# Two-stage kernel (talking-heads attention, then a squared-ReLU feed-forward): 64-row matmuls in four 64x64 tiles between 64x64 units, and a new order of TensorE's units

## The chip, the cores and the metric

The kernel runs on one core of a Trainium2 chip. The metric is device time in microseconds (us) of one execution, as the median of several runs; lower is better. The profile of one further execution is read beside it. In its rows PE is TensorE's matmuls, PEld its weight loads, DVE is VectorE, ACT ScalarE, POOL GpSimd, and SP the engine that issues part of the transfers. L1230 is line 1230 of the kernel.

## What is computed

```python
def _attn_ref(q, k, v, w_pre, w_post):          # q, k, v: 8 batches, 12 heads, 448 rows, 64 columns
    scores = scale * np.matmul(q, k.transpose(0, 1, 3, 2))
    scores = np.einsum('bhij,hg->bgij', scores, w_pre)
    scores = scores - np.max(scores, axis=-1, keepdims=True)
    attn = np.exp(scores)
    attn = attn / (np.sum(attn, axis=-1, keepdims=True) + 1e-09)
    attn = np.einsum('bhij,hg->bgij', attn, w_post)
    return np.matmul(attn, v)

def _moe_ref(x, w_in, w_out):                   # x: 3584 x 768, w_in: 768 x 2048, w_out: 2048 x 768
    h = np.maximum(x @ w_in, 0.0)
    return h * h @ w_out
```

The output of the attention, heads side by side, is the x of the feed-forward. Scores are mixed over heads before the softmax (w_pre) and after it (w_post).

## The kernel before

The 8 batches are worked through in overlap: while one batch is in attention, an earlier one is in the feed-forward. TensorE's work is cut into 966 units of one or a few dozen matmuls each. They fall into ten streams, each with a fixed order of its own:

- T (stream 0): transposes of q and k, 28 matmuls of 64x64 each. Two evacuations copy the result to `qkt`.
- QK (1): q times k transposed for one pair of heads and a tile of 128 (or, for the last tile of a batch, 64) rows, 448 columns. Two heads lie on the two halves of the 128 rows of the array, since a head has only 64 columns to contract over. `emit_QK`, matmul at L935. Its results are copied to `stage`, and from there SP moves them into the ring `dring`, where the 12 heads of five rows lie side by side.
- pre (2): mixes heads with `wk1`, 4 matmuls of 60 or 64 rows, two chunks at a time. L1004. ACT takes the exponential of the result, with row sums, into `pring` (L1022); DVE takes the reciprocals (L1046); POOL folds them into the weights of the second mix, `wk2s` (L1053).
- post (3): mixes heads after the softmax, 16 matmuls of 60 columns. L1085. Results are copied to `a2t`.
- AV (4): the product with v. One part (`avq`, L1142) uses 64x64 tiles, the rest (L1163) 128x64. Results are copied to `xt`.
- dir (5): batch 0's way to the mixed scores without the ring, full 128x128 matmuls. L883.
- F1 (6, 7): x @ w_in. Batches 0 and 1 use full matmuls (L1209), the later ones pairs of 64 rows (L1230): each unit, called a phase, contracts one half of the rows into one bank and the other half into another, and the second phase swaps them. ReLU and square follow on ACT and DVE (`h1t`, `h2t`).
- F2 (8, 9): h2 @ w_out, in the same paired form (L1351), the last two tiles of the last batch in full matmuls (L1300). The result goes to `osb` and out to memory.

A unit has a form, which the code calls its mode: "full" (128x128), "row" (two tiles of 64x128), "cols" (two of 128x64) or "quad" (four of 64x64). Where the form changes from one unit to the next, the planner adds a fixed time, `MODE_SWITCH`.

The order in which TensorE runs the units is written out by hand as a string, `ORDER`, of one digit per unit: the digit names the stream whose next unit comes. A planner, `_Plan`, lays the program out when the kernel is built: `run` takes units from the string, and at the same time chooses the order on all other engines by estimated costs and priorities, which engine (ACT or DVE) does each evacuation, and which of the eight banks of PSUM each group of results gets. `next_unit` gives the earliest start of the next unit, `_commit_pe` places it. So a new string also gives new queues on ACT, DVE, POOL and SP. Loads of q and k for a batch are released by certain pre units of the batch before; `load_v` and the moves into the ring are released in the same way.

The planner also counts TensorE's instructions and lets a unit wait where a block of them (`BLOCK`) would not have been fetched in its estimate (`fetch`, `fetch_wait`); each matmul is two instructions, the weight load and the matmul itself.

Of the kernel before, what the change touches and what calls it, by code (L numbers as in the profile page):

```python
# [27 lines left out]
INF = float("inf")  # L28
ORDER = (
    "0001155500055555555555555555513155553115531500335555555513155113555555513255555303203324"  # L30
    "2441310041137163162227676232273673322773316633176114244114222777662332766111671333673117"
    "2266720029333921293912812283383382400244411002671118123833381118132672226671336613367224"
    "2444223667311771133773020277622181382238338336721414441007763227766220066213831811183182"
    "2933913191119223922293193339242444221633611711713633622007223736221672137602106733720208"
    "1381118113822293931391339242244422381118133833382422444222636337117116116226336022073721"
    "7337201063621733720209323911191119322813831181338242444222919133933394222444228318333811"
    "1813622267317126362200733733621267200176322637317220091191119333922281813381118222831833"
    "3842244442444238631162020733733622267611713617227373376336420024441218128338202083391119"
    "1119392229192239111933813831384224442286133617222767316176316713762126733722293933392129"
    "81228338382424442238383338382227673667667736836464447767676776677677676899899889889899"  # L40
)


# [9 lines left out]
class _Task:  # L53

    __slots__ = ("name", "engine", "fn", "deps", "after", "cost", "prio", "sem", "seminc",
                 "semval", "end", "order", "nwait", "succs", "clock", "avail", "mode", "dma",
                 "done", "bias", "sync", "group", "instrs", "issued", "later", "two", "safe", "takes")

    def __init__(self, name, engine, fn, deps, after, cost, prio, sem, seminc, mode, dma,
                 group, instrs):  # L60
        self.name = name
        self.engine = engine
        self.fn = fn
        self.deps = []
        for d in deps:
            if d is not None and d not in self.deps:
                self.deps.append(d)
        self.after = [d for d in after if d is not None and d not in self.deps]
        self.cost = cost
        self.prio = prio  # L70
        self.sem = sem
        self.seminc = seminc
        self.semval = 0
        self.end = None
        self.clock = None
        self.mode = mode
        self.dma = dma
        self.sync = ()
        self.done = self.issued = False
        self.later = []  # L80
        self.two = False
        self.safe = None
        self.takes = ()
        self.bias = 0.0
        self.succs = []
        self.avail = 0.0
        self.group = group
        self.instrs = instrs
# [13 lines left out]
class _Plan:  # L102
# [144 lines left out]
        at = start + part * t.cost[PE][0]  # L247
        return max(0.0, self.fetched - at), at

    def _commit_pe(self, t, start):  # L250
        if t.mode != self.mode:
            self.mode = t.mode
        g = t.group
        if g is not None and g.banks is None:
            _, got = self.find(g.n, self.free[PE])
            g.banks = sorted(got)
            for i, readers in zip(g.banks, g.readers):
                for d in self.bank_users[i]:
                    if d not in t.deps:
                        t.deps.append(d)  # L260
                self.bank_users[i] = readers
                self.age += 1
                self.bank_age[i] = self.age
        stall, at = self.fetch_wait(t, start)
        if at is not None:
            self.fetched = at + stall + self.fetch(at + stall)
        for first, last, box in t.takes:
            s = self.n_slot % len(self.slots)
            self.n_slot += 1
            box.append(s)  # L270
            d = self.slots[s]
            self.slots[s] = last
            if d is None:
                continue
            first.deps.append(d)
            if d.done:
                first.avail = max(first.avail, d.end + SEM_LAT)
            else:
                first.nwait += 1
                d.succs.append(first)  # L280
        held, lat = t.cost[PE]
        t.cost = {PE: (held + stall, lat + stall)}
        self.instrs += t.instrs
        self._commit(t, PE, start)

    def next_unit(self, order, at):
        if at >= len(order):
            return None
        t = self.streams[int(order[at], 36)][0]
        if t.nwait:  # L290
            return None
        est = max(self.free[PE], t.avail)
        if t.group is not None and t.group.banks is None:
            est = max(est, self.find(t.group.n, self.free[PE])[0])
        if t.mode != self.mode:
            est = max(est, self.free[PE] + MODE_SWITCH)
        return (est, t) if est < INF else None

    def run(self, order=""):
        self.start()  # L300
        at = 0
        while True:
            best = None
            for t in self.ready:
                if t.engine == FLEX:
                    e = min(t.cost, key=lambda e: max(self.free[e], t.avail) + t.cost[e][1]
                            + (ACT_BIAS if e == ACT else t.bias if e == DVE else 0.0))
                else:
                    e = t.engine
                key = (max(self.free[e], t.avail), t.prio, t.order, t, e)  # L310
                if best is None or key[:3] < best[:3]:
                    best = key
            f = self.next_unit(order, at)
            d = self.dma_next()
            if d < INF and (best is None or d < best[0]) and (f is None or d < f[0]):
                self.dma_next(True)
                continue
            if f is not None and (best is None or f[0] <= best[0]):
                if self.warm_up is not None:
                    self.warm_up(f[0] - self.free[PE])  # L320
                    f = self.next_unit(order, at)
                self.streams[int(order[at], 36)].pop(0)
                at += 1
                self._commit_pe(f[1], f[0])
            elif best is not None:
                start, _, _, t, e = best
                self.ready.remove(t)
                self._commit(t, e, start)
            else:
                break  # L330
        assert not any(self.streams), "TensorE's work does not come to its end"
        assert len(self.committed) == len(self.tasks)
        self.span = max(t.end for t in self.tasks)
        return self.per_engine, self.committed


def bass_talking_heads_attention__then__ffn_squared_relu_kernel(
# [10 lines left out]
    B, H, S, D = q.shape  # L348
# [21 lines left out]
    NFT = F // 128  # L370
# [11 lines left out]
    with ExitStack() as es:  # L382
# [80 lines left out]
        def c_pe(t):  # L463
            return {PE: (t, t + 190.0)}
# [8 lines left out]

        events = {}

        def unit(s, name, fn, deps, ns, mode, group, mms):
            kind = name[:2]
            was = events.get(kind, 0.0)
            events[kind] = was + EVENTS.get(kind, 0.5)
            n = 2 * mms + int(events[kind]) - int(was)  # L480
            t = add(name, PE, fn, deps, c_pe(ns), 0, mode, group, n)
            s.append(t)
            return t

# [433 lines left out]
        def emit_QK(b, T):  # L918
# [8 lines left out]
            for p in ((0, 3, 1, 4, 2, 5) if n == 0 else range(0, NP, IT // w)):  # L927
                g = _Group(2)

                def fn_qk(eng, en, p=p, g=g):  # L930
                    r_ = None
                    for x, y in QUADS:
                        if y * w < IT:
# [6 lines left out]
                            )  # L940
                    return r_

                quad = w == PJ
                t_qk = unit(s_QK, "qk%d_%d_%d" % (b, T, p), fn_qk,
                            [trev[(b, p + y)] for y in range(IT // w)]
                            + [trev.get((b, p + y, 0)) for y in range(IT // w)],
                            205.0 if quad else 190.0, "quad" if quad else "row", g,
                            4 if quad else 2)
                t_qk.after += old
                for x, y in QUADS:  # L950
                    if y * w >= IT:
# [247 lines left out]
        def emit_F1(b, parts, t16, s_F):  # L1199
# [23 lines left out]
            for ph in range(2):  # L1223
                def fn_h(eng, en, ph=ph):
                    r_ = None
                    for ft in range(NFT):
                        for y in range(2):
# [7 lines left out]
                            )  # L1235
                    return r_

                t_h = unit(s_F, "h%d_%d_%d_%d" % (b, c0, t16, ph), fn_h,
                           [t for part in parts for t in xtev[(b, part)]]
                           + w_of[(0, t16 * NWP // NFFT)] + [before],  # L1240
                           NFT * (n / 2.4 + 4.3), "row", g, 2 * NFT)
                t_h.sync = [before]
                before = t_h
            f1_done(b, parts, t16, t_h)
# [86 lines left out]
        def emit_F2(b, tile, s, s_F):  # L1331
# [12 lines left out]
            for ph in range(2):  # L1344
                for q0 in range(0, NFFT, nk):
                    def fn_o(eng, en, q0=q0, ph=ph, g=g):
                        r_ = None
                        for t16 in range(q0, q0 + nk):
                            for y in range(2):
# [7 lines left out]
                                )  # L1357
                        return r_

                    sync = [t_o] if ph == 1 and q0 == 0 else []  # L1360
                    t_o = unit(s_F, "o%d_%d_%d_%d" % (b, tile, ph, q0), fn_o,
                               [sq_of[r][t] for r in reads for t in range(q0, q0 + nk)]
                               + [t for j in range(q0 * NWP // NFFT,
                                                   (q0 + nk - 1) * NWP // NFFT + 1)
                                  for t in w_of[(1, j)]] + sync,
                               nk * (FH / 2.4 + 3.7), "row", g, 2 * nk)
                    t_o.sync = sync
            f2_of[(b, tile)] = t_o
            for hh in range(2):
# [245 lines left out]
```

## Time and profile before

| | |
|---|---|
| median of 3 runs | 525.88 us |
| the three runs | 525.88, 528.05, 523.45 us |
| span of the profiled execution, first to last instruction | 522.0 us |
| TensorE matmuls, busy | 508.8 us |
| TensorE weight loads, busy | 322.6 us |
| ACT busy, DVE busy, POOL busy | 420.4, 398.6, 203.7 us |

The profiled execution has a span and no time of its own beside it, so its 522.0 us are set against the three runs: they lie 1.4 to 6.0 us above it. In the rows, the first numbers of a group are its busy time in us and the mean length of one instruction in ns; what stands behind the bar is idle time before the group and what ended it. In a timeline, a row is start, length, engine, line, operation, and the count of instructions merged into it. A form such as 64*128 is rows by columns of the array, and 64x448 the moving operand.

### The profile page before, as it was taken

The numbers are of one execution on the slowest core, as the hardware profiler recorded it, in microseconds if no ns is written. First come the engines' busy times: TensorE is split into PE (matmuls) and PEld (weight loads), VectorE is DVE, ScalarE is ACT, GpSimd is POOL, SyncE is SP. The second block draws the span as 40 slices with busy tenths as digits, with TensorE's granted clock in tenths as the row PEclk, the third lists the DMA queues.
The fourth block names the chain that finished last, engine by engine and source line by source line (L and its number), as shares of the span: only waits on it lengthen the run. The fifth ranks groups of instructions, "written<-read, shape, count | busy, mean of one in ns | idle before, by whom it ended". The sixth has DMA issues, their size and how long they took to land.

```text
span 522.0 us, 23220 instructions
## 1 busy us (share of the span) xinstructions
PE 508.8 (97%) x9632; PEld 322.6 (62%) x9632; DVE 398.6 (76%) x1002; ACT 420.4 (81%) x1208; POOL 203.7 (39%) x404
## 2 busy tenths in 40 slices
PE   8999899999999999999999999999999999999995
PEld 4456577567777565566556665566556565567963
DVE  6967689888988689977988669975888768867520
ACT  3689799889999899898988889988889786986311
POOL 9914345533651365134622357125712241241010
PEclk9999899999999999999999999999999999999999
DMA  8998999746894589657974679547954566541013
GB/s 159 196 216 174 183 173 197 169 110 137 169 182 108 138 169 178 139 114 159 165 146 97 143 169 180 122 93 155 188 99 89 137 143 117 114 114 37 4 30 98
DMA packets 82714, 71.95 MB, mean 138 GB/s; under 512 B 13578, under 2 KB 80090, under 8 KB 82602
## 3 DMA queue, kind: packets, MB, share of 16 engines
q0 software_dynamic: 36944, 32.81, 38.6%
q1 hardware_dynamic: 45370, 37.38, 30.0%
q8 instruction: 79, 1.29, 1.0%
q14 instruction: 33, 0.27, 0.2%
q10 hardware_dynamic: 288, 0.20, 0.2%
HBM read 45.70 MB, written 11.01 MB: 109 GB/s over the span
## 4 chain that ended last, share of the span: by engine, by line
PE 89%; ACT 5%; DVE 2%; POOL 1%; DMA 1%; issue 1%; ACTq 0%
PE ps L1351 26%; PE ps L1230 20%; PE ps L1085 8%; PE ps L1004 8%; PE ps L1209 7%; PE ps L935 6%; PE ps L1163 6%; PE ps L883 5%; PE ps L1300 2%; PE ps L786 2%; ACT pring L1022 2%; ACT stage L487 2%; DMA kraw<-in_k_dram 1%; POOL vraw L687 1%; PE ps L610 1%
## 5 line engine op out<-in xcount | busy, mean ns | idle before, releaser
L1022 ACT ACTIVATE pring<-ps 128x448 bf16<-128x448 f32 x360 | 191.1, 554 | 19.5 <-PE ps L1004 13.1
L1351 PE MATMUL ps<-w_out_sb,h2t 64*128 64x384 bf16 x1664 | 151.6, 323 | 0.0
L1053 POOL TENSOR_TENSOR wk2s<-wk2b,rinv 128x120 bf16<-128x120 bf16 (+1 forms) x179 | 69.8, 394 | 190.6 <-DVE rinv L1046 189.3
L488 DVE CAST a2t<-ps 128x480 bf16<-128x480 f32 (+1 forms) x199 | 121.5, 639 | 17.7 <-PE ps L1085 16.5
L1230 PE MATMUL ps<-xt,w_in_sb 64*128 64x448 bf16 (+2 forms) x1344 | 121.2, 323 | 0.0
L488 DVE CAST stage<-ps 128x448 bf16<-128x448 f32 (+1 forms) x175 | 104.1, 617 | 15.0 <-PE ps L935 13.3
L487 ACT ACTIVATE stage<-ps 128x448 bf16<-128x448 f32 (+1 forms) x185 | 93.8, 550 | 20.5 <-PE ps L935 19.8
L1351 PEld LDWEIGHTS ps<-w_out_sb,h2t 64*128 64x128 bf16 x1664 | 78.5, 94 | 49.4 <-issue 2.6
L487 ACT ACTIVATE a2t<-ps 128x480 bf16<-128x480 f32 (+1 forms) x169 | 89.6, 576 | 13.1 <-PE ps L1085 12.3
L1230 PEld LDWEIGHTS ps<-xt,w_in_sb 64*128 64x128 bf16 x1344 | 61.5, 94 | 39.9 <-PE ps L1004 1.9
L1383 POOL DMA_DIRECT2D out_dram<-osb x59 | 37.0, 633 | 111.5 <-ACT pring L1022 55.6
L1022 ACT ACTIVATION_READ_ACCUMULATOR pring<-ps 128x1 f32 x360 | 78.4, 218 | 0.0
L1085 PEld LDWEIGHTS ps<-wk2s,pring 60*128 60x128 bf16 x2880 | 55.7, 94 | 22.8 <-ACT pring L1022 3.5
L1085 PE MATMUL ps<-wk2s,pring 60*128 60x60 bf16 x2880 | 61.9, 187 | 1.1 <-POOL wk2s L1053 0.4
L1261 DVE TENSOR_SCALAR h1t<-ps 128x448 bf16<-128x448 f32 (+2 forms) x99 | 47.5, 486 | 17.3 <-PE ps L1230 9.9
L1004 PE MATMUL ps<-dring,wk 60*64 60x448 bf16 (+1 forms) x676 | 54.6, 362 | 3.5 <-ACT pring L1022 2.0
L1270 DVE TENSOR_TENSOR h2t<-h1t 128x448 bf16<-128x448 bf16 (+2 forms) x176 | 53.8, 336 | 1.4 <-ACT h1t L1260 0.8
L1046 DVE RECIPROCAL rinv<-rowsum 128x2 f32<-128x2 f32 (+1 forms) x184 | 28.9, 157 | 28.6 <-ACT pring L1022 27.6
L935 PE MATMUL ps<-qkt 64*128 64x448 bf16 (+1 forms) x360 | 49.2, 353 | 0.3 <-DVE qkt L488 0.3
L1260 ACT ACTIVATE h1t<-ps 128x448 bf16<-128x448 f32 (+2 forms) x77 | 34.5, 454 | 16.1 <-PE ps L1230 14.9
L1209 PE MATMUL ps<-xt,w_in_sb 128*128 128x228 bf16 (+1 forms) x384 | 43.2, 266 | 0.0
L1209 PEld LDWEIGHTS ps<-xt,w_in_sb 128*128 128x128 bf16 x384 | 35.5, 100 | 5.9 <-DVE h2t L1270 0.9
(64 smaller groups left out, 422.4 us busy)
## 6 DMA issues: line engine op xcount, KB each, us to landing
dring<-stage SPq DMA_DIRECT2D x309, 105.0 KB
out_dram<-osb POOLq DMA_DIRECT2D x45, 192.0 KB, 3.8
qraw<-in_q_dram POOLq DMA_DIRECT2D x42, 112.0 KB, 5.0
kraw<-in_k_dram POOLq DMA_DIRECT2D x42, 112.0 KB, 5.4
w_in_sb<-in_moe_w_in_dram POOLq DMA_DIRECT2D x8, 384.0 KB, 11.8
w_out_sb<-in_moe_w_out_dram POOLq DMA_DIRECT2D x8, 384.0 KB, 9.4
vraw<-in_v_dram POOLq DMA_DIRECT2D x21, 128.0 KB
vraw<-in_v_dram POOLq DMA_DIRECT2D x21, 96.0 KB
```

Source lines behind the costliest of these rows:

```text
L487: return eng.activation(o, i_, AF.Copy)
L488: return eng.tensor_copy(o, i_)
L935: r_ = eng.matmul(ps[y * w:(y + 1) * w, g.banks[x], 0:S], qkt[r0:r0 + 64, pb, p + y, 0, i0:i0 + w], qkt[r0:r0 + 64, pb, p + y, 1, :], star ...
L1004: r_ = eng.matmul(ps[64 * y:64 * y + 64, gr.banks[x], 0:S], wk1[64 * x:64 * x + 64 - R0 * x, :], dring[64 * x:64 * x + 64 - R0 * x, (g0 + ...
L1022: return eng.activation(pring[:, pr, 0:S], ps[:, gr.banks[x], 0:S], AF.Exp, accum_out=rowsum[:, rs, :])
L1053: return eng.tensor_tensor(wk2s[:, p0:p0 + n, :], i0.to_broadcast([128, n, PR]), rinv[:, p0:p0 + n, :].to_broadcast([128, n, PR]), ALU.mult)
L1085: r_ = eng.matmul(ps[:, gr.banks[x], o0:o0 + PR], pring[64 * x:64 * x + PR, pr + y, j0:j0 + 2 * PJ], wk2s[64 * x:64 * x + PR, pr + y, :], ...
L1209: r_ = eng.matmul(ps[:, g.banks[0], 0:n], w_in_sb[:, ft, t * 128:(t + 1) * 128], xt[:, ft, c0:c1], start=(ft == 0), stop=(ft == NFT - 1))
L1230: r_ = eng.matmul(ps[:, g.banks[x], 0:n], w_in_sb[64 * y:64 * y + 64, ft, t * 128:(t + 1) * 128], xt[64 * y:64 * y + 64, ft, c0:c1], start ...
L1261: return eng.tensor_scalar(h1t[:, box[0], 0:n], ps[:, g.banks[x], 0:n], 0.0, None, op0=ALU.max)
L1270: return eng.tensor_tensor(h2t[:, t16, o0:o0 + n], h1t[:, box[0], 0:n], h1t[:, box[0], 0:n], ALU.mult)
L1351: r_ = eng.matmul(ps[:, g.banks[hh], 0:FH], h2t[64 * y:64 * y + 64, t16, col:col + 128], w_out_sb[64 * y:64 * y + 64, t16, hh * FH:(hh + 1 ...
```

## The change

Units of QK (in the tiles of 128 rows), F1 and F2 that have the row form get a second way of running, with four 64x64 tiles: each 64x128 matmul is cut into two of 64 columns, so that the unit has twice as many matmuls and weight loads, into the same places of PSUM. The planner chooses for each unit when it places it. If the form at that moment is "row", the unit keeps the row form. Otherwise it looks ahead in the order for the next unit that has no choice; behind a quad unit it takes four tiles unless that next unit is in row form, and behind a full or cols unit it takes four tiles only where that next unit is quad. The post units, also in row form, have no such choice.

The order string is new from its 171st digit on. The costs that the planner counts for a unit are unchanged; the number of instructions goes up with the four tiles.

```diff
 ORDER = (
     "0001155500055555555555555555513155553115531500335555555513155113555555513255555303203324"
-    "2441310041137163162227676232273673322773316633176114244114222777662332766111671333673117"
-    "2266720029333921293912812283383382400244411002671118123833381118132672226671336613367224"
+    "2441310041137163162227676232273673322773316633176114244114222777662332766111671333761722"
+    "1366732290029231913932820018238333800422444218111812182338231776131673322771136663316624"
...
-    "81228338382424442238383338382227673667667736836464447767676776676677677676899899889889899"
+    "19288242444338338732728228228338367366773367746444767676676776767676686989898898899988"
 )
...
+    def tiling(self, order, at, t):
+        if t.flex is None or self.mode == "row":
+            return t.mode
+        seen = {int(order[at], 36): 1}
+        then = "row"
+        for c in order[at + 1:]:
+            s = int(c, 36)
+            n = seen.get(s, 0)
+            seen[s] = n + 1
+            if n >= len(self.streams[s]):
+                break
+            u = self.streams[s][n]
+            if u.flex is None:
+                then = u.mode
+                break
+        if self.mode == "quad":
+            return "row" if then == "row" else "quad"
+        return "quad" if then == "quad" else "row"
...
-    def _commit_pe(self, t, start):
-        if t.mode != self.mode:
-            self.mode = t.mode
+    def _commit_pe(self, t, start, mode=None):
+        self.mode = mode or t.mode
+        if self.mode != t.mode:
+            t.fn, more = t.flex
+            t.instrs += more
...
-        if t.mode != self.mode:
+        mode = self.tiling(order, at, t)
+        if mode != self.mode:
             est = max(est, self.free[PE] + MODE_SWITCH)
-        return (est, t) if est < INF else None
+        return (est, t, mode) if est < INF else None
...
+                def fn_qk4(eng, en, p=p, g=g):
+                    r_ = None
+                    for x, y in QUADS:
+                        r0, i1 = 64 * x, i0 + 64 * y
+                        r_ = eng.matmul(ps[64 * y:64 * y + 64, g.banks[x], 0:S],
+                                        qkt[r0:r0 + 64, pb, p, 0, i1:i1 + 64],
+                                        qkt[r0:r0 + 64, pb, p, 1, :], start=True, stop=True)
+                    return r_
...
+                def fn_h4(eng, en, ph=ph):
+                    r_ = None
+                    for ft in range(NFT):
+                        for y, z in QUADS:
+                            x = ph ^ y
+                            t = (t16 + x) * 128 + 64 * z
+                            r_ = eng.matmul(
+                                ps[64 * z:64 * z + 64, g.banks[x], 0:n],
+                                w_in_sb[64 * y:64 * y + 64, ft, t:t + 64],
+                                xt[64 * y:64 * y + 64, ft, c0:c1],
+                                start=(ph == 0 and ft == 0), stop=(ph == 1 and ft == NFT - 1),
+                            )
+                    return r_
...
-                           NFT * (n / 2.4 + 4.3), "row", g, 2 * NFT)
+                           NFT * (n / 2.4 + 4.3), "row", g, 2 * NFT, fn_h4)
...
+                    def fn_o4(eng, en, q0=q0, ph=ph, g=g):
+                        r_ = None
+                        for t16 in range(q0, q0 + nk):
+                            for y, z in QUADS:
+                                hh = ph ^ y
+                                r_ = eng.matmul(
+                                    ps[64 * z:64 * z + 64, g.banks[hh], 0:FH],
+                                    h2t[64 * y:64 * y + 64, t16, col + 64 * z:col + 64 * z + 64],
+                                    w_out_sb[64 * y:64 * y + 64, t16, hh * FH:(hh + 1) * FH],
+                                    start=(ph == 0 and t16 == 0),
+                                    stop=(ph == 1 and t16 == NFFT - 1),
+                                )
+                        return r_
```

`QUADS` is ((0, 0), (1, 1), (0, 1), (1, 0)): half of the rows, half of the columns.

More of the change, by code (lines that the diff above doesn't have):

```diff
@@ L30 @@
     "0001155500055555555555555555513155553115531500335555555513155113555555513255555303203324"
-    "2441310041137163162227676232273673322773316633176114244114222777662332766111671333673117"
-    "2266720029333921293912812283383382400244411002671118123833381118132672226671336613367224"
[L33 to L40, printed above, removed]
+    "2441310041137163162227676232273673322773316633176114244114222777662332766111671333761722"
+    "1366732290029231913932820018238333800422444218111812182338231776131673322771136663316624"
+    "2244427231676311771227671316733367202027677321812833662003832183620402443218121811381383"
+    "3932291292191342219321913393329422444231631631610023617132727233737321762136632006127272"
+    "0028318131811182292393139331924142143341282128238323284321444123733371611160207237363261"
+    "2626200733762116702071912191239113922383383138311821922192219434433932244144332821283383"
+    "3411821762161737107026226363261723722006236713373910209112912192381118331833382424442128"
+    "3138332824244243382171010737117326216236336327217621367327020610602833811832824244413913"
+    "1913191319219212922391393383282284244438361163621266121671337373262762712772217933933932"
+    "19288242444338338732728228228338367366773367746444767676676776767676686989899898899988"
 )
@@ L56 @@
                  "semval", "end", "order", "nwait", "succs", "clock", "avail", "mode", "dma",
-                 "done", "bias", "sync", "group", "instrs", "issued", "later", "two", "safe", "takes")
+                 "done", "bias", "sync", "group", "instrs", "issued", "later", "two", "safe", "takes",
+                 "flex")
     def __init__(self, name, engine, fn, deps, after, cost, prio, sem, seminc, mode, dma,
@@ L83, in __init__ @@
         self.takes = ()
+        self.flex = None
         self.bias = 0.0
@@ L323, in run @@
                 at += 1
-                self._commit_pe(f[1], f[0])
+                self._commit_pe(f[1], f[0], f[2])
             elif best is not None:
@@ L474, in bass_talking_heads_attention__then__ffn_squared_relu_kernel, with unit @@
         events = {}
-        def unit(s, name, fn, deps, ns, mode, group, mms):
+        def unit(s, name, fn, deps, ns, mode, group, mms, quads=None):
             kind = name[:2]
@@ L481, in unit @@
             t = add(name, PE, fn, deps, c_pe(ns), 0, mode, group, n)
+            if quads is not None:
+                t.flex = (quads, 2 * mms)
             s.append(t)
@@ L947, in emit_QK @@
                             205.0 if quad else 190.0, "quad" if quad else "row", g,
-                            4 if quad else 2)
+                            4 if quad else 2, None if quad else fn_qk4)
                 t_qk.after += old
@@ L1365, in emit_F2 @@
                                   for t in w_of[(1, j)]] + sync,
-                               nk * (FH / 2.4 + 3.7), "row", g, 2 * nk)
+                               nk * (FH / 2.4 + 3.7), "row", g, 2 * nk, fn_o4)
                     t_o.sync = sync
```

## The prediction

> **What bounds the kernel now.** I read four views in this order: the page's busy time and slices, the chain that ended last, the groups by line and shape, and then TensorE's timeline in narrow windows.
>
> ```profile
> span 522.0 us, 23220 instructions
> PE 508.8 (97%) x9632; PEld 322.6 (62%) x9632; DVE 398.6 (76%) x1002; ACT 420.4 (81%) x1208; POOL 203.7 (39%) x404
> PE 89%; ACT 5%; DVE 2%; POOL 1%; DMA 1%; issue 1%; ACTq 0%
> 84.60:150.00 65.40, 65.31 (x1403) 45.03 (x1396) 57.45 (x152) 59.72 (x180) 29.94 (x62) 1.00 0.77 155
> 250.00:350.00 100.00, 98.61 (x2002) 59.24 (x2000) 83.32 (x191) 89.80 (x254) 39.16 (x79) 1.00 0.70 139
> 450.00:512.00 62.00, 61.65 (x1128) 45.21 (x1125) 33.09 (x97) 31.81 (x94) 11.66 (x24) 1.00 0.25 59
> ```
>
> TensorE is the bound: 97% busy, 89% of the chain. The last three rows are stretches behind unit 170 of the order, which stands at 84.6 us; their columns are length, busy time of PE, PEld, DVE, ACT, POOL, granted clock, DMA share, GB/s. But a matmul's row is longer than its slot, so "busy" hides small losses. The slot is read from starts:
>
> ```profile
> 203.38 0.36 PE L1230 MATMUL ps<-xt,w_in_sb 64*128 64x448 bf16 x2
> 203.66 0.57 PE L1004 MATMUL ps<-dring,wk 64*64 64x448 bf16 x8
> 204.07 0.36 PE L935 MATMUL ps<-qkt 64*64 64x448 bf16 x4
> 204.36 0.36 PE L1230 MATMUL ps<-xt,w_in_sb 64*128 64x448 bf16 x2
> ...
> 134.69 0.54 PE L935 MATMUL ps<-qkt 64*128 64x448 bf16 x4
> ...
> 202.43 1.30 PE L1230 MATMUL ps<-xt,w_in_sb 64*128 64x448 bf16 x12
> ...
> 497.17 9.10 PE ps L1351 x112
> 506.27 10.52 PE ps L1300 x64
> ```
>
> I call a round the matmuls that run side by side: two in the 64x128 form, four in 64x64. Six F1 rounds (12 matmuls at 202.43) show 1.30 us; the last starts 0.35, one row's length, before that ends, and (1.30 - 0.35) / 5 = 0.19. Fifty-six F2 rounds run from 497.17 to the next piece of the chain at 506.27: 9.10 / 56 = 0.1625. Two row-form QK units: 0.54 - 0.35 = 0.19 apart. Now the changes of form: F1 to pre starts 203.66 - 203.38 = 0.28 after a round that needs 0.19, so 0.09 for the switch; quad QK back to F1 is 204.36 - 204.07 = 0.29, so 0.10. I take 0.095. Counting the order string of before against the unit lists gives 245 switches, 23.3 us. All units at such slots add up to 466 us (F1 146, F2 145, post 41, AV 34, pre 33, QK 30, direct scores 25, transposes 12); 5.3 us precede the first unit and 5.2 follow the last matmul. What is left, 522.0 - 466 - 23.3 - 10.5 = 22 us, are waits and late weights; measured start to start, about 10 us of them lie behind unit 170, the only part that the change reorders.
>
> **The change part by part.**
>
> *Fewer switches.* With the new string and its rule, 46 of 138 row-form QK units, 41 of the 112 row-form F1 units and 38 of the 104 row-form F2 units run in 64x64. Counting in the same way, switches fall from 245 to 228. The new string by itself, without the rule, would have 385; the old string with the rule 226. So the rule spends most of what it saves on a more mixed order, and only 17 x 0.095 = 1.6 us come off TensorE's path.
>
> *The rounds of these units.* 46x1 + 41x6 + 38x8 = 596 rounds of two matmuls become 596 of four. The same rows and columns of the array are used, so a round should keep its slot; a few of F1's have only 220 or 228 columns. Evidence:
>
> ```profile
> L935 PE MATMUL ps<-qkt 64*128 64x448 bf16 x276 | 41.4, 351 | 0.3 <-DVE qkt L488 0.3
> L935 PE MATMUL ps<-qkt 64*64 64x448 bf16 x84 | 7.8, 359 | 0.0
> L1351 PEld LDWEIGHTS ps<-w_out_sb,h2t 64*128 64x128 bf16 x1664 | 78.5, 94 | 49.4 <-issue 2.6 <-DVE osb L488 1.5 <-ACT xt L487 0.7
> L935 PEld LDWEIGHTS ps<-qkt 64*64 64x64 bf16 x84 | 2.5, 105 | 2.3 <-issue 0.5 <-ACT stage L487 0.4 <-DVE stage L488 0.3
> 203.88 0.12 PEld L935 LDWEIGHTS ps<-qkt 64*64 64x64 bf16 x4
> L786 PE MATMUL ps<-ident,kraw 64*64 64x64 bf16 x588 | 8.7, 194 | 0.5 <-DMA kraw<-in_k_dram 0.5
> ```
>
> The same QK matmul has both forms: 351 ns in 64x128, 359 in 64x64. The weight loads are 105 against 94 ns, but four start within 0.02 us of each other (four take 0.12 in all), and at 203.88 they run while pre's second round is in the array, so QK follows 0.19 later. The transposes show that four loads and four matmuls can pass in much less than a slot: 588 in 8.7 us of busy time, 4 x 8.7 / 588 = 0.06 a round at most. Bounds: no gain from below, since neither form has a shorter slot than 0.19; from above the two pre rounds at 203.66, which are 0.57 - 0.36 = 0.21 apart because their second weights came late, 0.02 x 596 = 12 us. I take 0: that lateness belongs to a unit one round long, and an F1 or F2 unit has its next weights at hand. The cover is a matmul of 0.16 to 0.19 over a load of 0.105; without it a round costs 0.10 more.
>
> The Trainium skill (TensorE: Matmul & The Clock Gate, What overlaps and what doesn't) says that a weight load overlaps matmuls in flight only where the row group differs. Four tiles occupy both row groups in every round, so by that rule each round would wait for its load, and the sum would end above before. The row at 203.88 speaks against it: loads into both row groups ran under matmuls of both.
>
> *More instructions.* 2 x 1192 = 2384 loads and matmuls are added to TensorE's stream.
>
> ```profile
> q8 instruction: 79, 1.29, 1.0%
> 264.76 0.10 PEld L1004 LDWEIGHTS ps<-dring,wk 64*64 64x64 bf16 x1 [0.37 <-ACT a2t L487]
> 265.40 0.11 PEld L1004 LDWEIGHTS ps<-dring,wk 60*64 60x64 bf16 x3 [0.54 <-issue]
> 265.40 0.38 PE L1004 MATMUL ps<-dring,wk 64*64 64x448 bf16 x4 [0.57 <-ACT a2t L487]
> ```
>
> TensorE has 2 x 9632 of them and 79 packets of 16 KB on the instruction queue: about 244 to a block. At 264.76 one load runs, and its own matmul comes 0.64 us later with nothing between them to wait for: as I read it, the next block had not come. 2384 / 244 makes 10 blocks more in the same time, so they must follow each other 12% faster. Bounds: 0 if all come in time (nearly all do now), and 10 x 0.64 = 6.4 us if every added block stalls like this one. I take 1.0, one or two such stalls, nearer the low end because this is the only one behind unit 170.
>
> *The new order.* No transfer, evacuation or semaphore kind is added, but all engines' queues are planned anew from the order: SP's moves into dring, POOL's loads (released by a pre of the batch before), folds and output writes, and the split of evacuations between ACT and DVE all shift with the units. What waits there now:
>
> ```profile
> PE ps L1004 <- ACT a2t L487: 0.6, 1, 0.6
> PE ps L786 <- DMA kraw<-in_k_dram: 0.5, 1, 0.5
> PE ps L1085 <- POOL wk2s L1053: 0.4, 1, 0.4
> PE ps L1085 <- DVE rinv L1046: 0.2, 1, 0.2
> ```
>
> I laid both strings out at the slots above, with no waits, and compared distances. From the pre that releases a load to its transpose the shortest were 3.5, 3.9 and 5.2 us, and become 4.6, 5.0 and 5.1: the kraw wait has more room. From the last post to avq the shortest grows from 0.9 to 1.6. From pre to post the shortest grows from 2.4 to 2.7, but the 5% point falls from 3.7 to 3.2, so wk2s and rinv are late more often. ACT's and DVE's work per 6 us is as dense as before (median 0.90 of two engines before, 0.93 after). Bounds: all 10 us gone, or as much again added. I take -1.0, the two longest waits of transfers and dependencies above (0.5 + 0.4), rounded.
>
> *Sum*, against the profiled execution: 522.0 - 1.6 + 0 + 1.0 - 1.0 = 520.4 us of span. The median of the three runs shown, 525.88, is 3.9 above that span, so the median becomes 525.88 - 1.6 = 524.3 us.
>
> **The rivals.**
> *The waits go.* If the order takes away 7 of the 10 us of waits, 525.88 - 1.6 - 7 + 1.0 = 518.3 us. For it: wider distances at the loads. Against: pre to post is tighter, and evacuation is as dense.
> *The fetch stalls (slower).* Every added block stalls 0.64 us: 525.88 - 1.6 + 6.4 - 1.0 = 529.7 us. It decides from 2.6 us on, four such stalls, where it has used up the switches and the waits. For it: F2 in 64x64 issues 64 instructions in 1.3 us where it issued 32. Against: post already issues 32 in 0.22 us and hardly ever stalls.
> *Rounds of four are longer (slower).* At 0.02 us each, 525.88 - 1.6 + 12 = 536.3 us; it decides from 1.6 / 596 = 0.003 us a round, which is why the slot matters more here than anything else. For it: 359 against 351 ns. Against: the start-to-start slots.
> *No overlap of loads within a row group (slower).* 596 x 0.105 = 63 us: 525.88 - 1.6 + 63 = 587 us. The load row at 203.88 all but excludes it. This is the result that the skill's rule named above would give.
>
> **How the numbers follow.** Forecast 0.69; waits go 0.15; fetch stalls 0.09; longer rounds 0.06; no overlap 0.01. The likeliest is 524.3 us. The range leaves out part of both tails: below it reaches 520.5, half of the way to the rival without waits and more; above 528.5, toward the fetch case. One per cent, 5.3 us, is about what a measurement of this kernel can tell from no change; the three runs shown span 4.6. Faster by over 1% needs most of the waits to go: 0.15. Slower by over 1% needs the fetch case nearly in full, or longer rounds: 0.13. Within 1%: 0.72.
>
> **What would show it.** F1 at the new 64x64 line with rounds of 0.19 start to start, F2 with 0.1625: the rounds are right; 0.20 or more: wrong. Weight loads there near 105 ns, four at once. 228 changes of form, each near 0.095. About 89 packets on the instruction queue; stalls between a load and its own matmul count the fetch price. A kraw wait before a transpose under 0.5 us and wk2s and rinv waits longer than 0.6 in sum would show the order as I read it. The prediction is wrong if the waits of DMA, ACT or DVE behind 84.6 us change by more than 4 us either way.

## The result

Over 20 runs of each, the median goes from 525.17 to 520.98 us; the ratio is 0.9925, 95% interval 0.9901 to 0.9949: 3.9 us less, 0.75%. The ratio leaves out runs in a slower state (two of the changed kernel's 20), so it is not quite the quotient of the two medians. Forecast were 524.3 us, 1.6 us less, within 1%; the measured median lies just above the lower end of the forecast's range, 520.5. The profiled execution of the changed kernel happens to be a long one: its span of 522.6 us is above the 522.0 of before. Two further profiles of it span 517.6 and 518.6, two further ones of before 524.1 and 522.3. So both kernels are read from three profiles here.

The page of the changed kernel, its groups by line and shape on TensorE (the second part of each row: busy us and mean ns of one), and its timeline, the last three rows from the third profile:

```profile
PE 507.3 (97%) x10824; PEld 339.5 (65%) x10824; DVE 403.2 (77%) x1011; ACT 419.9 (80%) x1199; POOL 204.7 (39%) x404
q8 instruction: 89, 1.46, 1.1%
...
L1279 PE MATMUL ps<-xt,w_in_sb 64*64 64x448 bf16 x936 | 50.5, 350 | 0.7 <-issue 0.7
L1265 PE MATMUL ps<-xt,w_in_sb 64*128 64x448 bf16 x492 | 52.5, 349 | 0.0
L1414 PEld LDWEIGHTS ps<-w_out_sb,h2t 64*64 64x64 bf16 x1216 | 37.8, 108 | 14.1 <-issue 0.6 <-DVE qkt L514 0.4 <-ACT xt L513 0.3
...
200.00 1.31 PE L1279 MATMUL ps<-xt,w_in_sb 64*64 64x448 bf16 x24
225.12 1.47 PE L1414 MATMUL ps<-w_out_sb,h2t 64*64 64x384 bf16 x32
243.22 1.47 PE L1414 MATMUL ps<-w_out_sb,h2t 64*64 64x384 bf16 x32
```

An F1 unit in four tiles has 24 matmuls in six rounds: (1.31 - 0.35) / 5 = 0.19. An F2 unit has eight rounds: (1.47 - 0.33) / 7 = 0.163. Both are the slots of the row form. There are ten packets more on the instruction queue. The trace has 228 changes of form, again near 0.095 us each.

What became longer shows in the waits of TensorE's matmuls behind 82 us. "Issue" means that the matmul waited for nothing that the profile shows. First the longest rows of the changed kernel's first profile (522.6 us):

```profile
PE ps L812 <- issue: 2.0, 1, 2.0
PE ps L1244 <- issue: 1.6, 2, 1.3
PE ps L1279 <- issue: 0.7, 1, 0.7
PE ps L1198 <- issue: 0.7, 1, 0.7
PE ps L1039 <- DVE h1t L1310: 0.7, 1, 0.7
PE ps L1120 <- issue: 0.4, 1, 0.4
```

and the second profile of before (524.1 us):

```profile
PE ps L786 <- DMA kraw<-in_k_dram: 1.4, 1, 1.4
PE ps L1085 <- issue: 1.3, 1, 1.3
PE ps L786 <- DMA qraw<-in_q_dram: 1.1, 1, 1.1
PE ps L786 <- issue: 0.6, 1, 0.6
PE ps L1085 <- POOL wk2s L1053: 0.4, 1, 0.4
```

Over three profiles of each, the rows of "issue" add up to 0, 1.9 and 1.9 us before, and to 5.6, 1.9 and 3.5 changed. The 0 has one exception: the list puts the pre at 265.40 us, 0.6, down to ACT.

What became shorter, and was not in the sum at all, shows in SP's last wait, for the output to land. Before, and then the changed kernel:

```profile
SPq L1565 <- DMA out_dram<-osb: 3.6, 1, 3.6
```

```profile
SPq L1628 <- DMA out_dram<-osb: 1.9, 1, 1.9
```

### The profile page after: what moved, and what is told of

Read it like the earlier page. It is cut to its first block, busy times and chain, and to the rows that moved or that the text cites. A ratio compares the mean times of both kernels' runs of the same rounds, so it can differ in the third digit from the quotient of the medians.

```text
span 522.6 us, 25583 instructions
## 1 busy us (share of the span) xinstructions
PE 507.3 (97%) x10824; PEld 339.5 (65%) x10824; DVE 403.2 (77%) x1011; ACT 419.9 (80%) x1199; POOL 204.7 (39%) x404
## 4 chain that ended last, share of the span: by engine, by line
PE 89%; ACT 4%; DMA 2%; issue 2%; POOL 1%; DVE 0%; SPq 0%; POOLq 0%; ACTq 0%
PE ps L1400 16%; PE ps L1265 11%; PE ps L1414 10%; PE ps L1120 8%; PE ps L1279 8%; PE ps L1039 8%; PE ps L1244 7%; PE ps L1198 6%; PE ps L909 5%; PE ps L961 4%; PE ps L1349 2%; PE ps L812 2%; PE ps L973 2%; ACT pring L1057 2%; DMA qraw<-in_q_dram 1%
## 5 line engine op out<-in xcount | busy, mean ns | idle before, releaser
L514 DVE CAST stage<-ps 128x448 bf16<-128x448 f32 (+1 forms) x192 | 114.4, 618 | 15.3 <-PE ps L961 6.5
L513 ACT ACTIVATE stage<-ps 128x448 bf16<-128x448 f32 (+1 forms) x168 | 87.6, 549 | 22.0 <-PE ps L961 10.9
L1400 PE MATMUL ps<-w_out_sb,h2t 64*128 64x384 bf16 x1056 | 95.9, 322 | 0.0
L1265 PE MATMUL ps<-xt,w_in_sb 64*128 64x448 bf16 (+2 forms) x852 | 70.8, 310 | 0.0
L1400 PEld LDWEIGHTS ps<-w_out_sb,h2t 64*128 64x128 bf16 x1056 | 49.8, 94 | 29.3 <-issue 1.0
L1039 PE MATMUL ps<-dring,wk 64*64 64x448 bf16 (+1 forms) x676 | 60.8, 361 | 2.3 <-ACT h1t L1309 1.5
L1414 PE MATMUL ps<-w_out_sb,h2t 64*64 64x384 bf16 x1216 | 57.9, 328 | 0.2 <-issue 0.2
L1279 PE MATMUL ps<-xt,w_in_sb 64*64 64x448 bf16 (+1 forms) x984 | 52.0, 345 | 0.7 <-issue 0.7
L1265 PEld LDWEIGHTS ps<-xt,w_in_sb 64*128 64x128 bf16 x852 | 39.1, 94 | 18.7 <-PE ps L1039 0.6
L1414 PEld LDWEIGHTS ps<-w_out_sb,h2t 64*64 64x64 bf16 x1216 | 37.8, 108 | 14.1 <-issue 0.6
```

What stands on the lines that cost most here:

```text
L513: return eng.activation(o, i_, AF.Copy)
L514: return eng.tensor_copy(o, i_)
L1039: r_ = eng.matmul(ps[64 * y:64 * y + 64, gr.banks[x], 0:S], wk1[64 * x:64 * x + 64 - R0 * x, :], dring[64 * x:64 * x + 64 - R0 * x, (g0 + ...
L1265: r_ = eng.matmul(ps[:, g.banks[x], 0:n], w_in_sb[64 * y:64 * y + 64, ft, t * 128:(t + 1) * 128], xt[64 * y:64 * y + 64, ft, c0:c1], start ...
L1279: r_ = eng.matmul(ps[64 * z:64 * z + 64, g.banks[x], 0:n], w_in_sb[64 * y:64 * y + 64, ft, t:t + 64], xt[64 * y:64 * y + 64, ft, c0:c1], s ...
L1400: r_ = eng.matmul(ps[:, g.banks[hh], 0:FH], h2t[64 * y:64 * y + 64, t16, col:col + 128], w_out_sb[64 * y:64 * y + 64, t16, hh * FH:(hh + 1 ...
```

## The experiments

**Second and third profiles.** No edit.

> The kernel before, unchanged, for a second profile. Theory A (the forecast's terms hold, and single profiles differ by stalls of instruction blocks and of loads): units and 245 switches take the same 466 + 23.3 us again, and what differs from the first profile is in single waits of 0.5 to 2.5 us at other places. Theory B (waits stand at fixed places of the order): the same places wait, each within 0.2 us; pre30 to pre32 at 54 us loses 2.1 us again and the pre at 263.5 us 0.64 us again.

> The changed kernel, unchanged, for a second profile. Its first profile (522.6 us) is 3.3 us above its median, and behind unit 170 it waits 18.0 us in all against 11.4 before. Theory A: the places that lost 0.9 to 2.2 us there (98.4, 148.1, 101.0, 311.2, 328.7, 385.7 us) are instruction blocks that came late, these differ from run to run, and a second profile waits some 3 us less, span 517 to 521. Theory B: they are waits that the order makes, and stay.

> The kernel before, a third profile. Theory A: waits that are the same in all profiles add up to about 9.5 us behind unit 170, 0 to 3 stalls at block boundaries there add 0 to 3 us, and 5.6 us follow the start of the last matmul. Rival: stalls as many as in the changed kernel, 2 to 7.

> The changed kernel, a third profile. Theory A: behind unit 170, waits that are the same in all profiles add up to about 8.4 us; 2 to 7 stalls at block boundaries of TensorE's instruction stream, at other places than in the two before, add 2 to 8 us. Rival: the same boundaries stall each time.

Measured: one run of each, 525.89 and 524.04 us before, 519.37 and 520.38 changed. I split the excess of each unit over its slot behind unit 170, transition by transition, into what all three profiles of a kernel share and what comes and goes. The shared part is 8.9 us before and 7.7 changed (1.3 less before rounding). For the part that varies, I numbered TensorE's instructions, loads, matmuls and waits, in the order of the program. Many of the longest gaps end exactly at an instruction whose number is 193 modulo 256 (in a few at 194, by the count of waits), and always 1.3 to 1.7 us after the last packet on the instruction queue had ended. Behind 82 us there are 1, 2 and 2 such gaps before, 0.5, 1.9 and 1.9 us above the slot in sum, and 7, 3 and 5 changed, 6.3, 2.1 and 3.6 us. The 0.64 us at 265.40 that the prediction read as a late block is one of them. Another, third profile of the changed kernel, matmuls and then weight loads:

```profile
145.29 0.65 PE L1244 MATMUL ps<-xt,w_in_sb 128*128 128x228 bf16 x5
147.21 0.56 PE L1244 MATMUL ps<-xt,w_in_sb 128*128 128x228 bf16 x4 [1.26 <-issue]
...
147.20 0.41 PEld L1244 LDWEIGHTS ps<-xt,w_in_sb 128*128 128x128 bf16 x5 [1.52 <-issue]
```

In the middle of one F1 unit, whose operands are all there, weights and matmuls stop together. So theory A holds in the main: stalls for a block of 256 instructions vary from run to run, and the changed kernel has more of them. The count I had set for before (0 to 3) and changed (2 to 7) was met; two places (98.5 and 146 to 148 us) recur in two profiles, so they are not wholly accidental. Of the six places that I had named as late blocks, four are at such boundaries. The one at 385.7 is not: it is a wait for DVE, and the third profile has it again.

The one at 101.0 is something else, the clock. An F2 unit of 32 matmuls, 1.47 us elsewhere, takes 2.71 there. Its row, and the stretch of half clock that it lies in (length, busy time of TensorE, granted clock, DMA share, GB/s):

```profile
100.98 2.71 PE L1414 MATMUL ps<-w_out_sb,h2t 64*64 64x384 bf16 x32
101.05:104.46 3.41, 3.41 (x58) 0.50 0.50 124
```

Before their last matmul, the six profiles have four such stretches of 3.41 us: one in each profile of before (from 57.65, 90.45 and 139.48 us on) and one in the changed kernel's first. Each opens within 1.3 us behind the end of a wait or stall in which TensorE started nothing for 1.6 to 2.3 us, but some waits of that length have none behind them. The matmuls inside take 3.4 to 3.5 us where the other profiles of the same kernel need 1.8 to 2.0, so one stretch costs 1.5 us more.

**The new order without the rule.**

The strings are written short here.

```diff
 # kernel before
-ORDER = (old)
+ORDER = (new)
```

> The new order without the rule: all QK, F1 and F2 units in row form, 385 switches, no added matmuls, 79 packets on the instruction queue. Theory A: 157 switches more than the changed kernel at 0.095 us = +14.9 us, less the stalls of added blocks (1 to 3 us), so 12 to 14 us above the changed kernel and 8 to 11 us above before, ratio 1.015 to 1.021. Rival, switches are partly hidden by waits that are there anyway: under 1.010. Rival, the new order waits less by itself: ratio under 1.010 with 385 switches still at 0.095 each in the trace.

Measured: ratio 1.0187 (1.0147 to 1.0226), 9.8 us above before and, by the two ratios, 13.7 above the changed kernel. The trace has 385 changes of form, and TensorE's list of waits has no row at all between 82 and 527 us: no stall of a block, no late load. These are four runs, and the 13.7 lie in the 12 to 14 expected: 157 switches at the price of the rows (157 x 0.095 = 14.9 us), less a part that the stalls of the rule's added instructions give back.

**The old order with the rule.**

```diff
 # changed kernel
-ORDER = (new)
+ORDER = (old)
```

> The order of before with the new rule: 226 switches (19 fewer than before), only 206 matmuls (412 instructions) added. Theory A, the gain is switches less stalls: -19 x 0.095 = -1.8 us, ratio 0.9965, and nearly no stalls added, 1 or 2 packets more on the instruction queue. Rival, the gain is the order's (fewer waits) and not the rule's: ratio 1.000 here. Rival, the rule is worth more than its switches: below 0.994.

Measured: ratio 1.0032 (0.9997 to 1.0067), 526.03 us. The 1.8 us of 19 fewer switches do not appear in the time, though the trace has 226. The interval holds the 1.000 of the first rival, but the timeline shows another reason than the rival's:

```profile
199.55 0.42 PE L812 MATMUL ps<-ident,kraw 64*64 64x64 bf16 x27
202.36 0.19 PE L812 MATMUL ps<-ident,kraw 64*64 64x64 bf16 x1 [2.39 <-issue]
```

Twenty-seven of 28 transposes run, and the last comes 2.4 us later. Three stalls behind 82 us, all at instructions 193 modulo 256, make 5.2 us, against 1.4 in the mean of before's profiles. Only 412 instructions were added, but they shift every boundary behind them, here two of the three into transposes, where 56 instructions pass in a quarter of a microsecond. "Nearly no stalls added" was wrong. This is one profile, of a run 1.7 us above the median, so the sum (3.8 us of stalls for 1.8 of switches) is rough.

**Instructions added without work.**

Here `n_pad` numbers the units. The four calls make two wait instructions a round in the trace (2256 more in all); the others ride on the second of them and on the weight load.

```diff
 # kernel before, fn_h and fn_o in row form, in three units of four
                     for ft in range(NFT):
+                        for _ in range(4 if n_pad % 4 else 0):
+                            eng.wait_ge(sem_w[0][0].handle, 32)
                         for y in range(2):
```

> The kernel before, with 2256 instructions added to TensorE's stream that compute nothing: in three of four row-form F1 and F2 units, two wait instructions a round on a load that landed long ago. Order, forms and 245 switches stay. The changed kernel adds 2384. Theory A, the number of TensorE instructions has a price through the blocks of 256 that are fetched: 87 to 88 packets on the instruction queue, stalls of 0.5 to 2.5 us at block boundaries, and 2 to 5 us over before (ratio 1.004 to 1.010), with F1 and F2 rounds still at 0.19 and 0.1625 us. Rival, added instructions are free: ratio 0.998 to 1.002. Rival, the waits themselves slow the rounds: rounds longer than 0.195 and 0.17 us in the trace.

Measured: ratio 1.1289 (1.1238 to 1.1339), 594.2 us, 88 packets on the instruction queue. The chain has the reason:

```profile
566.58 12.38 PE ps L1360 x112
```

The 56 F2 rounds, padded ones among them, take 12.38 us where they took 9.10. In the trace the added waits follow each other 0.106 us apart, so two of them and their round take 0.23. The second rival holds, and the time says nothing on the price of blocks (the trace has three longer stalls at instructions 193 modulo 256 behind 82 us: 2.0, 0.8 and 2.2 us from start to start). What the run gives is a price for a wait instruction.

**The old order with the new last digits.**

```diff
 # kernel before, end of ORDER
-...899889889899"
+...899898899988"
```

> The kernel before, with only the last 8 digits of its order changed, so that the last two F2 tiles end as in the changed kernel (results ready after units 3, 4, 6 and 8 of the eight, where they were after 3, 5, 6 and 8). Theory A, 1.7 us of the gain is the end of the program: from the last matmul's start to the end 3.9 us instead of 5.6, ratio 0.9967, nothing else changed. Rival, the shorter end comes from elsewhere in the new order: 5.6 us stays and the ratio is 1.000.

Measured: ratio 0.9967 (0.9931 to 1.0003), which is the number expected, but not for its reason: from the start of the last matmul to the end there are still 5.6 us, and SP waits 3.6 us for the output:

```profile
SPq L1565 <- DMA out_dram<-osb: 3.6, 1, 3.6
```

The interval holds 1, so the ratio settles nothing, and the trace rejects the theory in this form. The packets showed what I had missed: the last 16 KB packet on TensorE's instruction queue starts 2.0 to 2.1 us after the last matmul's start here and in the first profile of before, in the middle of the last output write, and a few packets of that write then come some 1.5 us after all others; in the changed kernel it starts at 3.0 to 3.4, when the write is all but over.

**Boundaries shifted by 64 and 128 instructions**, in the changed kernel and in the old order with the new last digits.

Two calls make one wait instruction, the other rides on the load.

```diff
 # fn_dir; 64 or 128
                 for p in ps_:
+                    if 6 * c + p < 64:
+                        eng.wait_ge(sem_hq.handle, 16)
+                        eng.wait_ge(sem_hq.handle, 16)
                     r_ = eng.matmul(ps[:, g.banks[0], 0:S],
```

> The changed kernel with 64 wait instructions on a load that landed long ago, one ahead of each of the first 64 matmuls of batch 0's direct scores (before 50 us; one such wait takes about 0.1 us of TensorE's sequencer in the padded run, and a matmul there has 0.19). So every later boundary of 256 instructions falls 64 instructions earlier in the work, and nothing else changes. Theory A, what a block costs depends on where its boundary falls: the stalls leave tr2_1_1 at 98.5, the units at 146 to 148, at 211 and 256 us, and others come, each at a boundary; the time moves by up to 3 us either way. Rival, the number of instructions alone counts: ratio to before as for the changed kernel, 0.990 to 0.995, with stalls as many. Rival, the stalls are waits of the order: they stay at the same units.

> As the one shifted by 64, with 128 wait instructions. Theory A: another set of stalls, time up to 3 us from the changed kernel's. Rivals as there. The end: if the shorter end of the new order (3.9 us behind the start of the last matmul) depends on where the last instruction block is fetched, it may become 5 to 5.6 us here; if it is the order of the last units alone, it stays 3.9.

> The old order with the new last 8 digits, and boundaries shifted by 64 instructions as above. With the last digits alone the end stayed 5.6 us, with a block fetched 2.0 us after the start of the last matmul while the last output is written; in the changed kernel that fetch comes at 3.0 to 3.4 and the end takes 3.9. Theory A, a fetch that meets the last write makes the end longer: 3.9 us if the fetch comes at 2.9 or later here, 5 to 5.6 if it comes at 2.0 to 2.5. Rival, the end depends on the order alone: 5.6 us whatever the fetch. Behind unit 170 the stalls at boundaries stand at other units than before.

> As the one shifted by 64, with 128 wait instructions. Theory A: the end is 3.9 us where the last block's fetch comes at 2.9 us or later behind the start of the last matmul, else 5 to 5.6; stalls at boundaries at again other units. Rival as there.

Measured: the changed kernel goes from 0.9925 to 1.0038 (1.0012 to 1.0064) with 64 instructions and to 1.0083 (1.0047 to 1.0119) with 128, 5.9 and 8.3 us lost, two to three times what I had allowed. The changed kernel itself was not timed beside them; its two single runs above, 519.37 and 520.38 us, stand at 0.991 and 0.992 of the medians of before beside them (524.11 and 524.73), so its gain is not of one series alone. The waits themselves cost nothing that shows: the direct-score units that hold them keep their median of 0.57 us for three matmuls. The waits of the one shifted by 128, from 45 us on:

```profile
PE ps L1201 <- issue: 3.4, 2, 2.6
PE ps L1268 <- issue: 2.9, 2, 1.6
PE ps L1123 <- issue: 1.9, 1, 1.9
PE ps L1247 <- ACT stage L513: 1.8, 1, 1.8
PE ps L964 <- issue: 0.7, 1, 0.7
```

The stalls stand at other units and again at instructions 193 modulo 256, and two stretches of half clock follow the first two of them, at 53.6 and 70.7 us. The packets on the instruction queue stay 89. So a block's price hangs on where its boundary falls, and the number of blocks is the smaller part of it: with both other placements that were tried the changed kernel's gain was gone. That the planner chose the one it has (it counts blocks of 256) fits, but was not tried.

The end was settled by the other two. With 64 the last block is fetched 2.2 us behind the last matmul's start, and the end takes 5.9 us. With 128 it is fetched at 2.9, the end takes 3.9, and SP's wait is:

```profile
SPq L1568 <- DMA out_dram<-osb: 1.9, 1, 1.9
```

Over all kernels with the new last digits, the end is 3.9 us where this fetch starts at 2.9 or later (7 profiles) and 5.6 to 5.9 where it starts at 2.0 to 2.2 (2). With the old last digits it is 5.3 to 5.9 in all 5, also in two where the fetch came at 3.1: there the output writes themselves end later (3.2 and 3.7 us, against 3.0). So the shorter end needs both, and one reading covers all 14 profiles: in the seven long ends the last 9 or 18 packets of the write start only as the fetch ends, and in the seven short ones no packet of the write comes behind it. What moves the fetch from 2.0 to 2.9 beyond the shift of the boundary is open. Times against before were 1.0025 (0.9993 to 1.0057) and 0.9984 (0.9948 to 1.0020). None of the kernels run was faster than the changed one.

## Why the prediction was right, and where its sum was not

The terms, forecast and measured as the mean of three profiles each, in us:

| term | forecast | measured |
|---|---|---|
| changes of form, 17 fewer | -1.6 | -1.6 |
| rounds of four tiles | 0 | 0 |
| instruction blocks, behind unit 170 | +1.0 | +2.6 |
| waits that repeat in all profiles | -1.0 | -1.3 |
| end behind the start of the last matmul | 0 | -1.6 |
| the rest, loads and the first 170 units | 0 | -1.3 |
| sum | -1.6 | -3.2 |

The three spans average 522.8 before and 519.6 changed, which is the -3.2; the 20 runs say -3.9. The prediction placed the start of unit 170 at 84.6 us in the first profile; it is 85.3, and nothing hangs on that. Of the last row, 0.9 lies ahead of unit 170, where the order on TensorE is the same: that part takes 81.7 to 85.3 us before and 82.3 to 82.4 changed. The stretches of half clock, 1.5 us each, account for about 1.0 of the row: three in the three profiles of before, one in the three changed. They come and go from profile to profile, so I do not credit them to the change; nor do I give the remaining 0.3 a cause.

*Fewer switches.* Right as a count and as a price; the run without the rule shows both.

*Rounds.* Right. Against this stands the rule of the Trainium skill (TensorE: Matmul & The Clock Gate, What overlaps and what doesn't) that loads overlap only matmuls of another row group. The F1 rounds of 0.19 with four loads in both row groups disagree with it; so did the row form of before, whose two loads also fill both row groups in rounds of 0.19. The Trainium skill (TensorEngine Tiling (Array Packing), Restrictions) also says that column tiling turns off the fast weight load. The trace agrees as far as 106 to 108 ns for 64 columns against 94 for 128; hidden under a matmul it costs nothing here.

*More instructions.* The mechanism was right and the size wrong: +2.6 for the +1.0, inside the bounds of 0 to 6.4. I had priced the number of blocks. The runs show that the place of the boundary weighs more: moving it by 64 instructions cost more than the change brings, and with the old order 412 added instructions ate the switches' gain. The forecast also took the first profile for the usual case, with one stall of 0.64; the other two had 1.9 each.

*The new order.* About right as a number, -1.3 for -1.0, but only half as a mechanism. The prediction had the loads of k and q with more room, and indeed no profile of the changed kernel has such a wait. It also had wk2s and rinv late more often, since the distance from pre to post shrinks at its 5% point, and yet counted wk2s's 0.4 us as gained. The two posts that wait for rinv (at 314.8 us) and wk2s (at 475.8) lose 0.4 and 0.5 us in all three profiles of before, and no post stands in the changed kernel's lists with either. So that reading of the distances was wrong, and the number owes part of its fit to luck. Why these waits went is not shown.

*What the sum left out* is the end. I took the 5.2 us behind the last matmul as given, because no unit stands in it. Its last wait, for the output to land, was 3.6 us with 2.4 to 2.7 us from issue to landing in the list of transfers; that it was longer than the transfer was the row to ask about. This missing 1.6 and the 1.6 by which the blocks were sized too small cancel, which is luck; the gap to the -3.2 of the profiles is then mostly in the rest, and so in the clock. The 22 us that the prediction called waits and late weights also hold one stretch of half clock, from 57.65 us on.

The rivals: the waits did not go (1.3 of 10 us), rounds did not grow, and the fetch stalls fell far short of the 6.4 us that would have ended on the other side. The shifted kernels show that they could have: the same change with its boundaries 128 instructions earlier is slower than before.

## What to carry to other kernels

Where an engine issues hundreds of short instructions, its instruction stream is a transfer too: number the instructions, look for gaps with no releaser that recur at the same remainder, and take any edit that adds or removes instructions ahead of a dense stretch as a shift of all boundaries behind it. Compare at least two profiles of each kernel before a wait is called the order's, look at the granted clock behind each long stall, and read the end of the program as a stage of its own. A change of form of TensorE is worth counting, but a rule that saves switches by adding instructions pays only as far as the blocks come in time.

## What the runs showed of the hardware that was not expected

- Where a block of TensorE's instructions came late, the first of them ran 1.3 to 1.7 us after its packet had ended, and TensorE started nothing, weight load or matmul, for up to 2.9 us (the changed kernel shifted by 64, at 54.7 us).
- Behind some stalls and waits of 1.6 us and more the granted clock is 0.50 for 3.41 us, and the matmuls there take 1.5 us longer in sum.
- Wait instructions on TensorE follow each other 0.106 us apart even when their value was reached long ago, while four 64x64 weight loads start within 0.02 us: 2256 such waits within F1 and F2 cost about 69 us, while 128 of them, one to a matmul of 0.19 us, left those units' lengths as they were.
- Where the last instruction block was fetched during the last output write, the write's last packets started only as the fetch ended, and the end took 5.3 to 5.9 us instead of 3.9.
